# Taking PSUM banks in aligned pairs, with one instruction over two banks, in a two-layer attention and MLP kernel

## The chip, the cores and the metric

One core of one Trainium2 chip. The metric is the device time of one execution in microseconds (us), median of several.

The engines, as the profile names them: PE is TensorE's matmuls, PEld its weight loads, DVE is VectorE, ACT is ScalarE, POOL is GpSimd. The granted clock in a view is the share of its full clock at which TensorE ran.

## The reference

Two layers, each linear attention followed by a gated MLP, both on a layer norm of x and both added to x. x is 2048 x 576 in bf16 (16 tiles of 128 rows), 32 heads of 18, hidden width 4608.

```python
def _A_ref(x, wqkv, w_phi, wo):              # attention; shapes cut
    q, k, v = ...                            # x @ wqkv, split in heads of 18
    pq = einsum("bhsd,hdf->bhsf", q, w_phi)
    pk = einsum("bhsd,hdf->bhsf", k, w_phi)
    phi_q = concat([softmax(pq), softmax(-pq)])
    phi_k = concat([softmax(pk), softmax(-pk)])
    kv = einsum("bhsf,bhsd->bhfd", phi_k, v)
    z  = einsum("bhsf->bhf", phi_k)
    num = einsum("bhqf,bhfd->bhqd", phi_q, kv)
    den = einsum("bhqf,bhf->bhq", phi_q, z)[..., None] + 1e-6
    return (num / den) @ wo
def _B_ref(x, w_gate, w_up, w_down):         # the MLP
    return ((x @ w_gate) * (x @ w_up)) @ w_down

x = x + _A_ref(_layernorm(x), ...); x = x + _B_ref(_layernorm(x), ...)   # layer 1
x = x + _A_ref(_layernorm(x), ...); x = x + _B_ref(_layernorm(x), ...)   # layer 2
```

The softmax of -pk needs the minimum of each head where that of pk needs the maximum. This is where the two-bank instructions come in.

## The kernel before

The kernel is built by a greedy scheduler in Python. Tasks (`t_v`, `t_ain`, `t_down` and so on) ask for buffers and hand over lists of instructions; at each step the builder takes the instruction that can start first by its own table of durations. So **the order of the instructions on every engine follows from durations, priorities and the moment at which a task gets a buffer**.

PSUM is one pool `pb` of eight banks. A request for n banks gets those that came free longest ago:

```python
        names, n = r[1], r[2]
        cand = []
        for nm in names:
            p = self.pools[nm]
            for idx in p["free"]:
                cand.append((p["rel_time"][idx], nm, idx))
        if len(cand) < n:
            return False
        cand.sort()
        ...                                   # the first n of them
```

A bank counts as free once the builder has placed the instruction that reads it last. `rel_time` says when that instruction ends, which can lie ahead. A matmul into such a bank waits for that reader.

Layer 1 takes three banks at the very start for its kv sums and gives them back at the end of its attention. Five banks are left for everything else in this stage:

```python
    def t_layer1(self):
        gots = yield ("acqn", ["pb"], 3)
        s.kvb = [g_[1] for g_ in gots]
```

Who asks for what in that stage: a transpose or a product of the weight fuse (w_phi is multiplied into the k and q weights at the start) takes one bank, half a v projection takes one, a k projection takes two, for the two halves (288 wide each) of its row of 576:

```python
    def softmax_front(self, st_, pz, Wm, km, crit, ...):
        gots = yield ("acqn", ["pb"], 2, True)
        banks = [g_[1] for g_ in gots]
        yield from s.proj(st_, Wm, km, banks)            # the matmuls
        for h in range(2):                                # ACT: one cast for each bank
            yield ("ops", "act", [... e.copy(psb[:, pz, 288*h:288*h+288], s.ps[:, bank, 0:288]) ...])
        ops = [... e.tensor_reduce(mxmn[:, pz, 0, :], p3, AX.X, ALU.max) ...]
        for h in range(2):                                # DVE: one minimum for each bank
            ops.append(... e.tensor_reduce(mxmn[:, pz, 1, 16*h:16*h+16], pv, AX.X, ALU.min) ...)
        ...
        for h in range(2):                                # DVE: one subtraction for each bank
            ops.append(... e.tensor_tensor(d2h, pv, mnbh, ALU.subtract) ...)
        yield ("ops", "dve", ops)
        for bank in banks:
            yield ("rel", "pb", bank)
```

The scaling of a row by its layer norm (`xln`) may go to POOL or ACT in layer 1 and to DVE only on a fast path (six rows in all: two just ahead of each layer's first gate/up matmul, two between the layers):

```python
            yield ("alt", [(eng, [...]) for eng, dur in
                 (("pool", (800, 200)[:2 - fast]), ("dve", (400,)))[:1 + fast]] + ([("act", act)] if boot else []))
```

## Time and profile before

| | before |
|---|---|
| median of 3 runs | 1115.49 us |
| span of the profiled run | 1113.9 us |
| first Wk projection (k) on PE starts | 14.19 us |
| first gate/up matmul starts (layer 1's kv sums and its first rows of attention are done) | 117.8 us |
| last gate/up matmul of layer 1 starts | 599.5 us |
| first gate/up matmul of layer 2 starts | 653.3 us |

The busy shares, the busy time by stretch and the tail of the profile are shown in the prediction.

### The profile page before, as it was taken

How to read it: one execution, taken by the hardware profiler on the slowest of the kernel's cores; microseconds unless marked ns; L12 is line 12 of the kernel's file. 1: busy time of each engine (PE TensorE's matmuls, PEld its weight loads, DVE VectorE, ACT ScalarE, POOL GpSimd, SP SyncE). 2: the span in 40 equal slices, each digit the busy share in tenths (PEclk: the TensorE clock that was granted, in tenths of full speed). 3: DMA queues.
4: the chain of work that ended last, by engine and by line, in shares of the span. 5: the costliest groups of instructions: out<-in, count | busy, mean ns of one | idle time of the engine just before them, and what ended most of it. 6: DMA issues, size and time to landing. Idle time of an engine off the chain costs nothing.

```text
span 1113.9 us, 33734 instructions
## 1 busy us (share of the span) xinstructions
PE 1069.7 (96%) x15280; PEld 835.1 (75%) x15342; DVE 588.4 (53%) x1184; ACT 374.4 (34%) x862; POOL 313.3 (28%) x334
## 2 busy tenths in 40 slices
PE   5788999999999999999999899999999999999998
PEld 4565886868687786869687678696969696969685
DVE  7788744647375564646453675444535353524231
ACT  7786631414133241414232463131313030402120
POOL 4885512424152432413220252121212030300000
PEclk9899999999999999999999999999999999999999
DMA  8494227273542616371523313717272726362604
GB/s 175 114 314 157 32 47 197 47 204 47 151 97 79 158 39 186 47 204 26 152 75 98 96 24 47 214 36 215 35 215 35 205 46 191 58 180 49 179 26 139
DMA packets 185002, 129.07 MB, mean 116 GB/s; under 512 B 103322, under 2 KB 183706, under 8 KB 183706
## 3 DMA queue, kind: packets, MB, share of 16 engines
q1 hardware_dynamic: 184858, 126.91, 44.4%
q8 instruction: 120, 1.97, 0.7%
q14 instruction: 24, 0.20, 0.0%
HBM read 100.75 MB, written 2.36 MB: 93 GB/s over the span
## 4 chain that ended last, share of the span: by engine, by line
PE 83%; DVE 7%; ACT 4%; DMA 3%; POOL 2%; issue 1%; SPq 0%; DVEq 0%; POOLq 0%; ACTq 0%
PE ps L1427 47%; PE ps L1497 20%; PE ps L1001 6%; PE ps L1500 4%; PE ps L989 3%; PE ps L1288 2%; DMA wdr<-in_B_w_down_dram 1%; PE ps L1169 1%; DVE ss L1116 1%; DVE dd L1048 1%; POOL dd L1127 1%; ACT hT L1473 1%; DVE mxmn L1034 1%; DVE hT L1475 1%; DVE mxmn L1029 1%
## 5 line engine op out<-in xcount | busy, mean ns | idle before, releaser
L1427 PE MATMUL ps<-xT,Wu 64*128 64x256 bf16 x4608 | 582.2, 269 | 0.0
L1427 PE MATMUL ps<-xT,Wg 64*128 64x256 bf16 x4608 | 579.8, 269 | 0.8 <-ACT xT L971 0.8
L1427 PEld LDWEIGHTS ps<-xT,Wu 64*128 64x128 bf16 x4608 | 431.8, 94 | 22.4 <-DVE hT L1475 1.6
L1427 PEld LDWEIGHTS ps<-xT,Wg 64*128 64x128 bf16 x4608 | 427.2, 94 | 27.0 <-issue 3.3
L1473 ACT CAST hT<-ps 128x512 bf16<-128x512 f32 x288 | 168.0, 583 | 567.8 <-PE ps L1427 526.6
L1475 DVE TENSOR_TENSOR hT<-ps,hT 128x512 bf16<-128x512 f32 x288 | 196.9, 689 | 216.1 <-ACT hT L1473 215.3
L1497 PE MATMUL ps<-wdr,hT 128*128 128x512 bf16 x913 | 237.3, 380 | 0.9 <-DMA wdr<-in_B_w_down_dram 0.9
L1427 PE MATMUL ps<-xT,Wr 64*128 64x256 bf16 x1152 | 190.0, 269 | 0.0
L1500 PE MATMUL ps<-wdr,hT 128*128 128x64 bf16 x960 | 185.0, 193 | 3.1 <-DMA wdr<-in_B_w_down_dram 0.4
L1497 PEld LDWEIGHTS ps<-wdr,hT 128*128 128x128 bf16 x960 | 93.8, 98 | 110.8 <-DMA wdr<-in_B_w_down_dram 2.5
L1127 POOL TENSOR_TENSOR dd<-dd,ss 128x576 bf16<-128x576 bf16 x119 | 136.8, 1172 | 124.9 <-ACT ss L1123 121.0
L1098 POOL TENSOR_TENSOR dd<-xT,mxq 128x576 bf16<-128x576 bf16 x56 | 63.9, 1163 | 320.6 <-DVE mxq L1094 320.6
L1522 DVE TENSOR_TENSOR x_sb<-ps,x_sb 128x512 bf16<-128x512 f32 x32 | 22.0, 687 | 225.6 <-PE ps L1500 225.6
L961 POOL TENSOR_SCALAR xln<-x_sb,nmean,rstd 128x576 bf16<-128x576 bf16 x104 | 62.5, 607 | 172.9 <-ACT rstd L950 108.8
L1116 DVE TENSOR_REDUCE ss<-dd 128x64 f32<-128x1152 bf16 x61 | 82.1, 1347 | 31.6 <-ACT dd L1110 31.5
L1500 PEld LDWEIGHTS ps<-wdr,hT 128*128 128x128 bf16 x960 | 94.3, 98 | 0.0
L1427 PEld LDWEIGHTS ps<-xT,Wr 64*128 64x128 bf16 x1152 | 82.8, 94 | 5.2
L1108 ACT ACTIVATE dd<-dd 128x576 bf16<-128x576 bf16 x61 | 41.7, 684 | 47.6 <-DVE dd L1048 30.9
L1039 POOL TENSOR_TENSOR dd<-psb,mxmn 128x576 bf16<-128x576 bf16 x26 | 30.2, 1163 | 80.6 <-DVE mxmn L1029 80.6
L1497 PE MATMUL ps<-wdx,hT 128*128 128x512 bf16 x177 | 50.8, 380 | 0.0
L933 DVE BATCH_NORM_STATS2 st<-x_sb 128x6 f32<-128x288 bf16 x120 | 46.0, 446 | 2.8 <-DMA x_sb<-in_A_x_dram 2.7
L1001 PE MATMUL ps<-Wo,oT 64*128 64x288 bf16 x504 | 44.0, 283 | 0.8
(123 smaller groups left out, 968.9 us busy)
## 6 DMA issues: line engine op xcount, KB each, us to landing
wdr<-in_B_w_down_dram SPq DMA_DIRECT2D x240, 288.0 KB, 3.5
wdx<-in_B_w_down_dram SPq DMA_DIRECT2D x48, 288.0 KB, 3.4
Wg<-in_B_w_gate_dram SPq DMA_DIRECT2D x4, 1152.0 KB, 16.4
Wu<-in_B_w_up_dram SPq DMA_DIRECT2D x4, 1152.0 KB, 18.5
x_sb<-in_A_x_dram SPq DMA_DIRECT2D x8, 288.0 KB, 3.1
out_dram<-x_sb SPq DMA_DIRECT2D x16, 144.0 KB, 2.3
Wraw<-in_A_wqkv_dram SPq DMA_DIRECT2D x8, 144.0 KB, 2.8
xT<-xln SPq DMA_TRANSPOSE x58, 2.6
```

Of the source, the lines that this page charges most:

```text
L933: ops.append(Op(d_dve(288), (lambda e, j=j, h=h, src=src: e.bn_stats(st[:, sl[j], 6 * h:6 * h + 6], src)), reads=rd, writes=[("st", sl[j], ...
L961: em = [(lambda e, j=j, a=a, b=b, c=c: e.tensor_scalar(xln[:, sl[j], a:b], x_sb[:, ss[j], c:c + b - a], s.nmean[:, sl[j]:sl[j] + 1], rstd[ ...
L1001: out.append(Op(61, (lambda e, h=h, k=k, st=(i == 0 and k == 0), sp=(i == 1 and k == 3): e.matmul(s.ps[:, banks[h], 0:N], L[r, k, :], Wm[r ...
L1098: yield ("ops", "pool", [Op(1150, (lambda e, d=d, mb=mb: e.tensor_tensor(d, p3, mb, ALU.subtract)), reads=[("xT", st_), ("mq", mq, br)], w ...
L1108: yield ("ops", "act", [Op(590, (lambda e: e.activation(de2, de2, ACTF.Exp, scale=-1.0)), reads=s.ddk(sm, 1), writes=s.ddk(sm, 1))])
L1116: Op(1320, (lambda e: e.tensor_reduce(ss[:, sm, :].rearrange("p (b g) -> p b g", b=2), e4, AX.X, ALU.add)), reads=s.ddk(sm, 0) + s.ddk(sm, ...
L1127: yield ("alt", [(eng, [Op(dur, (lambda e, ev=ev, rb=rb: e.tensor_tensor(ev, ev, rb, ALU.mult)), reads=s.ddk(sm, br) + [("ss", sm)], write ...
L1427: out.append(Op(54.3, (lambda e, bank=bank, cs=cs, lhsT=lhsT, rhs=rhs, st=st, sp=sp: e.matmul(ps[:, bank, cs].rearrange("p (a n) -> p a n" ...
L1473: yield ("ops", "act", [Op(540, (lambda e, gb=gb, p=p: e.copy(hT[:, p, :], ps[:, gb, :])), reads=[("gu", gb)], writes=[("hT", p)] + (s.raw ...
L1475: yield ("ops", "dve", [Op(625, (lambda e, ub=ub, p=p: e.tensor_tensor(hT[:, p, :], ps[:, ub, :], hT[:, p, :], ALU.mult)), reads=[("gu", u ...
L1497: ops.append(Op(d_pe(512), (lambda e, lhsT=lhsT, bank=bank, slot=slot, fi=fi, f=f: e.matmul(ps[:, bank, 0:512], lhsT, s.wslot(slot)[:, fi, ...
L1500: ops.append(Op(d_pe(64) + 3, (lambda e, lhsT=lhsT, sl=sl, slot=slot, fi=fi, f=f: e.matmul(ps[:, Z, 64 * sl:64 * sl + 64], lhsT, s.wslot(s ...
```

## The change

The intent: fewer, longer DVE and ACT instructions. Banks 2i and 2i+1 are adjacent in PSUM, so one instruction can read both. To have such a pair, banks are given by a new rule, and with it come four more edits. The diff, cut to its core:

```diff
+        if names[0] == "pb":
+            got = self._banks(r[2] if r[0] == "acqn" else 1)
+            if got is None:
+                return False
+    def _banks(self, n):
+        p = self.pools["pb"]
+        free, rel = set(p["free"]), p["rel_time"]
+        got = []
+        while n >= 2:                         # the pair demand
+            pairs = [i for i in range(0, 8, 2) if i in free and i + 1 in free]
+            if not pairs:
+                return None
+            i = min(pairs, key=lambda i: max(rel[i], rel[i + 1]))
+            got += [i, i + 1]
+            free -= {i, i + 1}
+            n -= 2
+        if n:                                 # the single rule
+            if not free:
+                return None
+            i = min(free, key=lambda i: ((i ^ 1) in free, rel[i]))
+            got.append(i)
+        return got
 ...
-        self.fq = 3                           # when the q weight is fused
-        self.fqs = 2
+        self.fq = 1
+        self.fqs = 1
 ...                                           # DVE may scale rows in layer 1
-  ("dve", (400,)))[:1 + fast]] + ...
+  ("dve", (400,) if fast else (400, 200)))[:1 + (fast or boot)]] + ...
 ...                                           # merges; the same for q cast, den, multiply, adds to x
-        for h in range(2):
-            ... e.copy(psb[:, pz, 288*h:288*h+288], s.ps[:, bank, 0:288])
+        pv = s.two(banks, 288)                # = self.ps[:, banks[0]:banks[0] + 2, 0:288]
+        ... e.copy(psb[:, pz, :].rearrange("p (t n) -> p t n", t=2), pv)
-        for h in range(2): ops.append(Op(370, ... ALU.min ...))
+        ops.append(Op(690, (lambda e: e.tensor_reduce(mn3, pv4, AX.X, ALU.min)), ...))
 ...                                           # last down phase: the last 3 chunks tile by tile
+        NR = NF - CH * s.NLAST * last
+        for sl in range(2):
+            for f in range(NR, NF):
+                yield ("ops", "pe", mm(f, sl))
+            if sl == 0 and last:
+                yield ("go", s.t_bepi(L, b, 0, X, ZZ[0], True), 11, "bepi%d" % b)
```

Below, its parts are called the **pair demand** (two banks must be an aligned pair), the **single rule** (a single bank is taken where its partner is taken, whenever that bank comes free), the **merges**, the **split** (of the last down phase, which also takes a fourth bank; the 64 wide add of a tile now comes before the 512 wide one), the **norms** (rows scaled by DVE in layer 1) and the **early fuse**.

## The prediction

> **What bounds the kernel now.** I read the page's busy shares first, then busy time by stretch, then the groups by shape, then the timeline at the three places where TensorE waits, and the chain that ended last.
>
> ```profile
> PE 1069.7 (96%) x15280; PEld 835.1 (75%) x15342; DVE 588.4 (53%) x1184; ACT 374.4 (34%) x862; POOL 313.3 (28%) x334
> ```
>
> TensorE is busy for 96% of the span and no other engine is near that. So what an instruction on VectorE or ScalarE costs matters only where TensorE waits for it. I cut the span by what TensorE does: attention of layer 1 ahead of the first gate/up matmul (0 to 117.85), gated block of layer 1, the passage between the layers (619 to 653.3), gated block of layer 2. Columns: stretch, its length, then busy us with instruction counts of PE, weight loads, DVE, ACT, POOL, then granted clock, DMA share, GB/s.
>
> ```profile
> 14.00:28.00 14.00, 10.83 (x69) 7.18 (x70) 12.85 (x38) 10.71 (x33) 7.74 (x10) 0.87 0.87 155
> 28.00:56.00 28.00, 20.56 (x169) 14.42 (x166) 22.20 (x47) 19.88 (x53) 22.34 (x23) 0.83 0.46 113
> 56.00:84.00 28.00, 23.73 (x221) 18.22 (x222) 24.48 (x44) 22.98 (x64) 24.95 (x23) 0.94 0.96 317
> 84.00:103.30 19.30, 14.88 (x124) 10.62 (x122) 17.78 (x31) 13.32 (x34) 11.38 (x10) 0.91 0.36 139
> 103.30:117.85 14.55, 13.91 (x139) 10.26 (x137) 10.96 (x27) 9.09 (x23) 4.50 (x5) 1.00 0.34 107
> 118.00:618.00 500.00, 497.39 (x7487) 388.55 (x7514) 271.87 (x537) 157.81 (x365) 149.58 (x158) 1.00 0.44 108
> 619.00:653.30 34.30, 28.87 (x268) 22.21 (x266) 26.50 (x59) 20.06 (x52) 9.58 (x8) 1.00 0.08 24
> 653.30:1084.00 430.70, 427.37 (x6477) 342.24 (x6506) 187.06 (x365) 107.92 (x216) 77.08 (x82) 1.00 0.45 113
> ```
>
> The two gated stretches hold 930.7 us, of which TensorE idles 2.61 + 3.33 = 5.9: nothing that shortens DVE or ACT work can gain more there. Between 14 and 103.3 us DVE is 87% busy (77.3 of 89.3), POOL 74% and TensorE 78% at a clock of 0.83 to 0.94: there VectorE, with GpSimd close behind in the middle, sets the pace. In the passage TensorE idles 5.4 of 34.3 us, behind a serial chain through DVE, ACT and POOL. After the last matmul (begun at 1109.63) come the adds and the store, some 4 us. These three places hold all there is to win.
>
> **What the Trainium skill says.** "Perfetto Trace Analysis", section Optimizing Scalar/DVE Operations, gives a data-access overhead per instruction of about 125 ns for DVE on PSUM and 51 ns for ScalarE on PSUM; it says that grouping helps a saturated engine, and that splitting may help one that is not saturated but causes bubbles elsewhere. Both halves bear on this change. The trace gives less for DVE than 125 ns (next part) and about as much for ACT. "PSUM — Partial Sum Buffer", section Terms, has one bank as 2 KiB per partition and one matmul output within one bank: the matmuls stay as they are, and two adjacent banks are one regular pattern for a reader. No run so far shows that such a read costs nothing extra; I assume it.
>
> **Cost of one merge.**
>
> ```profile
> L1363 DVE TENSOR_TENSOR x_sb<-ps,x_sb 128x288 bf16<-128x288 f32 x56 | 25.4, 454 | 6.0 <-PE ps L1001 4.9
> L1522 DVE TENSOR_TENSOR x_sb<-ps,x_sb 128x512 bf16<-128x512 f32 x32 | 22.0, 687 | 225.6 <-PE ps L1500 225.6
> L1473 ACT CAST hT<-ps 128x512 bf16<-128x512 f32 x288 | 168.0, 583 | 567.8 <-PE ps L1427 526.6 <-PE ps L1001 39.0
> L1026 ACT CAST psb<-ps 128x288 bf16<-128x288 f32 x56 | 20.4, 400 | 18.7 <-PE ps L1001 15.3 <-PE ps L989 3.4
> ```
>
> DVE: (687-454)/224 = 1.04 ns per element, so 576 elements should take 687 + 64 x 1.04 = 753 ns. ACT: (583-400)/224 = 0.82, so 583 + 52 = 635 ns. Against these stand pairs as the timeline has them (start, length of both, group):
>
> ```profile
> 626.55 0.81 DVE L1048 TENSOR_TENSOR dd<-ps,mxmn 128x288 bf16<-128x288 f32 x2
> 628.55 0.68 ACT L1026 CAST psb<-ps 128x288 bf16<-128x288 f32 x2
> ```
>
> Two back to back overlap, so a pair is 0.81, not 0.89, on DVE and 0.68, not 0.80, on ACT. A merge saves 0.055 us of DVE and 0.045 us of ACT, far less than a whole instruction. It also loses something: a cast of bank 1 began while bank 2 was still filling, so where a cast is on the path, 0.40 after the last matmul becomes 0.64.
>
> **Part by part.** The instruction lists of both builds (neither times anything) say what moves.
>
> 1. Layer 1 up to the gated block. DVE: 36 minima and 36 subtractions become 18 and 18: -36 x 0.055 = -2.0 us. Seven of the 16 normalisations (rows of 576 and 64; 0.43 us from the 576 row, and I take 0.15 for the 64) move to DVE: +4.1. Three weight casts leave it, -1.2. In sum about +0.9 us for DVE. POOL loses three normalisations of 0.82 + 0.39 us, -3.6; ACT loses four of 0.87 + 0.29 + 0.24, -5.6, and about -1.0 from merged casts. The moved work lands before 50 us, where DVE has some room (12.85 of 14, 22.2 of 28) and POOL less. So the merges hardly relieve the bound engine; it is the balance that gets better. DVE idles 12.0 us from 14 to 103.3, in part behind ACT and POOL. I choose 1.5 us of that as regained. At the end one q projection fewer stands before the first gate/up matmul, so that this waits for the last cast of xT (116.59 + 0.69) rather than for TensorE at 117.85: -0.5. Together -2.0.
> 2. That q projection, and one from the passage, go into the first gated block of each layer. A layer-2 block lasts 57.04 us (chain, gate/up starts at 771.95 and 828.99): 9 x 4.04 gate/up, 72 x 0.245 down, 2 x 0.62 attention numerator; 1.8 remains for two projections on half rows, 0.9 each. So +1.8 for the two.
> 3. Passage. Three chunks of two rows, six steps of one tile, 6 x 0.245 = 1.5 us of matmuls now stand behind tile 0's end, so its add and layer norm start 1.5 earlier. The new list puts tile 1's adds between tile 0's mean and its normalisation: tile 0's scaling starts near 620.2, not 621.40: -1.2. The merged cast gives 0.24 back: -1.0 at the softmax, and everything is serial from there to the kv matmuls at 637.68. Then transposes of tile 0 go ahead of tile 1's numerator (0.62): -0.6. One q projection less in front of the last transposes: -0.4. Together -2.0.
> 4. End. In
>
> ```profile
> 1109.58 0.69 DVE L1522 TENSOR_TENSOR x_sb<-ps,x_sb 128x512 bf16<-128x512 f32 x1 [16.13 <-PE ps L1500]
> 1110.19 0.21 DVE L1524 TENSOR_TENSOR x_sb<-ps,x_sb 128x64 bf16<-128x64 f32 x1
> 1110.32 0.68 DVE L1522 TENSOR_TENSOR x_sb<-ps,x_sb 128x512 bf16<-128x512 f32 x1
> 1110.92 0.21 DVE L1524 TENSOR_TENSOR x_sb<-ps,x_sb 128x64 bf16<-128x64 f32 x1
> ```
>
> all four adds come behind TensorE. Now only one 512 wide add does: 1109.85 (last matmul done, my estimate) + 0.69 = 1110.55 in place of 1111.13: -0.6.
>
> The other merges (denominator, multiply, adds, q casts inside gated blocks) lie beside a TensorE that does not wait: 0. Sum: -2.0 + 1.8 - 2.0 - 0.6 = -2.8. The constants that moved too (when the q weight is fused, normalisations allowed on DVE) look like the order being tuned again for the new lengths; for that I take 1.2 us more. 1115.49 - 4.0 = 1111.5.
>
> **Rivals.** (a) Aligned pairs run short. Layer 1 keeps three banks for kv through its attention; five remain, two pairs and a single, and a single v projection that breaks a pair would make a k projection wait while two banks are free. For it: TensorE waits on releases by casts there already. Against: singles take the odd bank first, and before it needed two of five as well. It would add 2 to 5 us in layer 1: 1114 to 1117. (b) A two-bank read costs DVE extra, or the casts' lost overlap is felt at each tile: 16 x 0.24 = 3.8 us more at worst, which eats the gain: 1115. (c) DVE stays the bound in layer 1 and the moved normalisations lengthen it by their 0.9 us; passage and end still gain: about 1114. (d) Balance is worth more than I took: all 12 us of DVE idling can't go, but half can: 1106.
>
> **Range and chances.** The three runs before spread by 2.8 us, so 1 us either way is the median's own. With (d) at one end and (a) to (c) at the other: 1106 to 1115.5. Faster by over 2% needs 1093.2, 22 us off, more than half of all TensorE idling: 0.02. Slower by 2% needs 1137.8, thus pair shortage in the gated blocks, whose matmul order is unchanged but for two projections: 0.01.
>
> **What would show it.** Right: merged DVE instructions of 0.74 to 0.77 us and casts of 0.63 to 0.65; first gate/up matmul at 115 to 116.5; passage near 32 us, end of matmuls to end of span 0.6 shorter; PE busy total within 3 us of 1069.7; gated stretches idle as before. Wrong: the first gate/up after 118 with TensorE waiting for DVE releases (a); merged instructions over 0.80 (b); idle over 8 us in the gated stretches.

## More of the kernel before

A change in how buffers are given moves instructions all over the stage.

One view that the prediction did not show belongs here. It is the timeline of PE at the start: start, length, line and operation, output and inputs, count, and in brackets the idle time before and what ended it.

```profile
5.21 1.33 PE L835 MATMUL ps<-ident,Wraw 128*126 128x128 bf16 x10 [5.21 <-DMA Wraw<-in_A_wqkv_dram]
7.07 0.64 PE L887 MATMUL ps<-BDphi,WT 126*128 126x126 bf16 x5 [0.53 <-ACT WT L838]
7.51 0.77 PE L835 MATMUL ps<-ident,Wraw 128*126 128x128 bf16 x5
...
14.19 2.56 PE L989 MATMUL ps<-Wk,xT 128*128 128x288 bf16 x10 [1.93 <-ACT Wk L900]
```

L835 are transposes of the raw weight, five to a bank. Ten of them run in one go, into two banks, and PE does not wait for the cast (L838) of the first bank before it fills the second.

## The result, and the profile after

The changed kernel takes 1121.53 us (median of 4 runs, 1120.37 to 1122.29), the kernel before 1114.97 us in the runs beside it (4 runs, 1113.39 to 1117.24). The ratio is 1.0056, 95% interval 1.0036 to 1.0077: within 2%, but slower by some 6 us, where 4 us less had been forecast, and outside the range.

| start on PE, profiled runs | before | after | difference |
|---|---|---|---|
| first Wk projection | 14.19 | 17.80 | +3.6 |
| first gate/up matmul | 117.8 | 124.6 | +6.8 |
| first gate/up matmul of layer 2 | 653.3 | 660.5 | +7.2 |
| end of span | 1113.9 | 1120.3 | +6.4 |

So **the whole loss lies ahead of the first gate/up matmul**, and half of it is there at 17.8 us. The granted clock does not explain it: up to the first gate/up matmul it was 0.91 before and 0.96 after. The page's first line and the busy time by stretch after (columns as in the prediction):

```profile
PE 1075.7 (96%) x15358; PEld 816.6 (73%) x15358; DVE 578.8 (52%) x1023; ACT 369.4 (33%) x797; POOL 311.0 (28%) x328
```

```profile
0.00:14.00 14.00, 5.29 (x38) 3.80 (x38) 7.54 (x26) 7.00 (x17) 3.57 (x15) 1.00 0.69 186
14.00:28.00 14.00, 9.97 (x62) 6.34 (x62) 11.91 (x30) 8.30 (x22) 6.16 (x8) 1.00 0.52 101
56.00:84.00 28.00, 20.39 (x169) 13.92 (x167) 26.84 (x41) 18.75 (x48) 19.09 (x18) 0.94 0.79 249
84.00:103.30 19.30, 15.41 (x140) 10.89 (x138) 18.64 (x22) 14.83 (x35) 16.22 (x15) 1.00 0.54 225
0.00:124.50 124.50, 90.29 (x750) 63.27 (x750) 101.22 (x180) 80.36 (x195) 76.29 (x83) 0.96 0.58 170
124.60:627.40 502.80, 501.95 (x7544) 385.17 (x7545) 265.07 (x467) 159.18 (x343) 147.92 (x156) 1.00 0.44 108
```

and two stretches of the kernel before that the prediction did not show:

```profile
0.00:14.00 14.00, 5.45 (x50) 4.71 (x50) 8.88 (x31) 9.60 (x24) 5.96 (x19) 0.98 0.74 192
0.00:117.85 117.85, 89.36 (x762) 65.42 (x764) 97.14 (x213) 85.57 (x226) 76.87 (x88) 0.91 0.63 180
```

161 DVE instructions are gone and 9.6 us of its busy time. But up to the first gate/up matmul DVE is busy for 101.2 us where it had been 97.1. By its account, 4.1 of the 6.8 us lost there are more work and 2.7 are more idling, though which instructions fall before that mark differs a little. In the gated stretch PE idles 0.85 of 502.8 us, so nothing is lost there. In the first 14 us PE got 38 instructions instead of 50, though nothing in this stretch is merged. The timeline of PE there after the change:

```profile
5.36 0.79 PE L865 MATMUL ps<-ident,Wraw 128*126 128x128 bf16 x5 [5.36 <-DMA Wraw<-in_A_wqkv_dram]
7.12 0.80 PE L865 MATMUL ps<-ident,Wraw 128*126 128x128 bf16 x5 [0.97 <-ACT WT L868]
...
11.46 0.79 PE L865 MATMUL ps<-ident,Wraw 128*126 128x128 bf16 x5 [0.80 <-ACT WT L868]
...
17.80 2.58 PE L1019 MATMUL ps<-Wk,xT 128*128 128x288 bf16 x10 [0.41 <-ACT Wk L930]
```

The transposes now come five at a time, and the second five wait 0.97 us for the cast of the first five: both go into the same bank. The banks that the two builders gave, in order, show why:

```
before: kv [0,1,2]; then singles 3 4 5 6 7 3 4 5 6 3 7 4 5 6 3;   first k [4,7]
after:  kv [0,1,2]; then singles 3 3 4 3 3 5 6 3 7 3 3 4 5 3 3;   first k [6,7]
```

Bank 3 is the one whose partner is held by the kv sums, so the single rule always likes it best, even while its reader is still at work: it is 9 of the 15 singles after and 4 before.

The merged instructions came out as forecast. The groups by shape (busy us, mean ns of one):

```profile
L1383 DVE TENSOR_TENSOR x_sb<-ps,x_sb 128x576 bf16<-128x576 f32 x28 | 21.0, 751 | 8.7 <-PE ps L1031 8.7
L1062 DVE TENSOR_REDUCE mxmn<-ps 128x32 f32<-128x576 f32 x28 | 20.9, 748 | 0.0
L1056 ACT CAST psb<-ps 128x576 bf16<-128x576 f32 x28 | 17.9, 638 | 21.4 <-PE ps L1031 13.4 <-PE ps L1019 7.9
```

A DVE merge is 0.75 us (forecast 0.753) and a cast 0.638 (0.635). The timeline of DVE shows what this saves, and where it goes:

```profile
33.69 0.74 DVE L1058 TENSOR_REDUCE mxmnx<-psbx 128x32 f32<-128x576 bf16 x1
34.35 0.74 DVE L1062 TENSOR_REDUCE mxmnx<-ps 128x32 f32<-128x576 f32 x1
35.02 0.73 DVE L1058 TENSOR_REDUCE mxmnx<-psbx 128x32 f32<-128x576 bf16 x1
...
42.30 0.75 DVE L1058 TENSOR_REDUCE mxmn<-psb 128x32 f32<-128x576 bf16 x1 [4.55 <-ACT psb L1056]
```

The merged minimum takes 35.02 - 34.35 = 0.67 us from start to start, a pair before took 626.55 - 625.82 = 0.73. But two tiles' minima come together, and then DVE stands still for 4.55 us for the cast of the next k projection. At this place DVE waits. Later it does not: from 56 to 103.3 us it is busy for 26.84 + 18.64 = 45.5 of 47.3 us (96%; before 24.48 + 17.78 = 42.3, 89%), so there DVE still sets the pace, more than before.

The norms came out dearer than forecast. Before, DVE has only the six 576-wide rows of the fast path (2.6 us, 428 to 429 ns each); after:

```profile
L991 DVE TENSOR_SCALAR xln<-x_sb,nmean,rstd 128x576 bf16<-128x576 bf16 x13 | 7.2, 554 | 2.8 <-ACT rstd L980 2.8
L991 DVE TENSOR_SCALAR xln<-x_sb,nmean,rstd 128x64 bf16<-128x64 bf16 x7 | 5.0, 719 | 0.3
```

The seven that moved cost 7.2 - 2.6 + 5.0 = 9.6 us, not 4.1: 64 elements take longer than 576 do at best. POOL is at work beside them at those times. Three of the seven come late, where DVE has no room:

```profile
60.51 1.46 DVE L991 TENSOR_SCALAR xln<-x_sb,nmean,rstd 128x576 bf16<-128x576 bf16 x2
64.69 3.47 DVE L991 TENSOR_SCALAR xln<-x_sb,nmean,rstd 128x576 bf16<-128x576 bf16 x4
```

The Trainium skill, "SBUF — State Buffer", section Who interferes with whom, says that DVE in a 2-port mode and GpSimd exclude each other for a whole instruction; that fits the lines of the seven, but run a4 below could not confirm it.

The end, timeline of DVE:

```profile
1115.11 0.23 DVE L1564 TENSOR_TENSOR x_sb<-ps,x_sb 128x64 bf16<-128x64 f32 x1 [14.73 <-PE ps L1523]
1115.31 0.69 DVE L1562 TENSOR_TENSOR x_sb<-ps,x_sb 128x512 bf16<-128x512 f32 x1
1116.58 0.22 DVE L1564 TENSOR_TENSOR x_sb<-ps,x_sb 128x64 bf16<-128x64 f32 x1 [0.57 <-PE ps L1523]
1116.78 0.69 DVE L1562 TENSOR_TENSOR x_sb<-ps,x_sb 128x512 bf16<-128x512 f32 x1
```

Tile 0's adds are over before PE ends (last matmul 1116.36 + 0.38 = 1116.74), as intended. From there to the end of the span it is 3.56 us, before it was 1113.9 - (1109.63 + 0.19) = 4.08: 0.5 us gained.

### The profile page after: what moved, and what is told of

It reads as the page before. It is cut to its first block, busy times and chain, and to the rows that moved or that the text cites. A ratio compares the mean times of both kernels' runs of the same rounds, so it can differ in the third digit from the quotient of the medians.

```text
span 1120.3 us, 33573 instructions
## 1 busy us (share of the span) xinstructions
PE 1075.7 (96%) x15358; PEld 816.6 (73%) x15358; DVE 578.8 (52%) x1023; ACT 369.4 (33%) x797; POOL 311.0 (28%) x328
## 4 chain that ended last, share of the span: by engine, by line
PE 85%; DVE 5%; DMA 3%; ACT 1%; POOL 0%; issue 0%; SPq 0%
PE ps L1448 50%; PE ps L1521 20%; PE ps L1031 7%; PE ps L1523 3%; PE ps L1312 2%; DMA wdr<-in_B_w_down_dram 2%; PE ps L1019 1%; DVE ss L1140 1%; PE ps L1193 1%; DVE dd L1071 1%; DMA oT<-dd 1%; DMA wdx<-in_B_w_down_dram 0%; DVE xln L991 0%; DVE mxmn L1062 0%; POOL dd L1151 0%; DVE mxmn L1058 0%
## 5 line engine op out<-in xcount | busy, mean ns | idle before, releaser
L1521 PE MATMUL ps<-wdr,hT 128*128 128x512 bf16 x960 | 245.9, 380 | 1.3 <-DMA wdr<-in_B_w_down_dram 1.1
L1448 PE MATMUL ps<-xT,Wr 64*128 64x256 bf16 x1152 | 162.5, 269 | 0.0
L1564 DVE TENSOR_TENSOR x_sb<-ps,x_sb 128x64 bf16<-128x64 f32 x32 | 7.0, 220 | 234.2 <-PE ps L1523 234.2
L991 POOL TENSOR_SCALAR xln<-x_sb,nmean,rstd 128x576 bf16<-128x576 bf16 x98 | 59.7, 615 | 178.3 <-ACT rstd L980 173.0
L1448 PEld LDWEIGHTS ps<-xT,Wr 64*128 64x128 bf16 x1152 | 61.1, 94 | 6.8
L1132 ACT ACTIVATE dd<-dd 128x576 bf16<-128x576 bf16 x61 | 41.6, 682 | 44.7 <-DVE dd L1071 35.9
L1521 PE MATMUL ps<-wdx,hT 128*128 128x512 bf16 x192 | 54.3, 380 | 0.1
L1134 ACT ACTIVATE dd<-dd 128x576 bf16<-128x576 bf16 x61 | 41.0, 671 | 0.0
## 6 DMA issues: line engine op xcount, KB each, us to landing
Wg<-in_B_w_gate_dram SPq DMA_DIRECT2D x4, 1152.0 KB, 14.2
```

Source lines behind the costliest of these rows:

```text
L991: em = [(lambda e, j=j, a=a, b=b, c=c: e.tensor_scalar(xln[:, sl[j], a:b], x_sb[:, ss[j], c:c + b - a], s.nmean[:, sl[j]:sl[j] + 1], rstd[ ...
L1132: yield ("ops", "act", [Op(590, (lambda e: e.activation(de2, de2, ACTF.Exp, scale=-1.0)), reads=s.ddk(sm, 1), writes=s.ddk(sm, 1))])
L1448: out.append(Op(54.3, (lambda e, bank=bank, cs=cs, lhsT=lhsT, rhs=rhs, st=st, sp=sp: e.matmul(ps[:, bank, cs].rearrange("p (a n) -> p a n" ...
L1521: ops = [Op(d_pe(512), (lambda e: e.matmul(s.ps[:, bank, 0:512], lhsT, s.wslot(slot)[:, fi, 0:512], start=(f == 0), stop=(f == NF - 1))), ...
```

## The experiments

Eighteen kernels were run. First their results in one table, then each group with its edits and expectations. "Wk", "g/u" and "g/u end" are the starts, in the profiled run, of the first Wk projection, the first gate/up matmul and the last gate/up matmul of layer 1. Each run was timed beside the kernel before on the same chip (medians there 1114.08 to 1115.34 us).

| run | what it is | median us | ratio to before (95%) | Wk | g/u | g/u end |
|---|---|---|---|---|---|---|
| before | | 1114.97 | 1 | 14.2 | 117.8 | 599.5 |
| after | all parts | 1121.53 | 1.0056 (1.0036 to 1.0077) | 17.8 | 124.6 | 607.6 |
| a1 | after, no norms | 1125.77 | 1.0092 (1.0076 to 1.0109) | 19.3 | 128.5 | 611.9 |
| a2 | after, old fuse | 1122.40 | 1.0062 (1.0047 to 1.0077) | 17.7 | 127.1 | 609.1 |
| a3 | after, neither | 1125.69 | 1.0087 (1.0072 to 1.0102) | 19.3 | 127.9 | 610.1 |
| a4 | after, norms strided | 1122.41 | 1.0062 (1.0047 to 1.0077) | 18.0 | 125.8 | 608.7 |
| b4 | before + bank rule | 1127.70 | 1.0123 (1.0106 to 1.0140) | 19.4 | 128.7 | 611.0 |
| b5 | before + split | 1111.82 | 0.9981 (0.9966 to 0.9996) | 13.9 | 117.5 | 598.2 |
| a5 | a3, adjacent pairs | 1143.83 | 1.0270 (1.0254 to 1.0285) | 16.9 | 135.3 | 611.2 |
| a6 | a3, old banks | 1112.16 | 0.9984 (0.9969 to 0.9999) | 14.1 | 119.0 | 599.2 |
| c1 | a3, pair preferred | 1130.55 | 1.0137 (1.0123 to 1.0151) | 19.3 | 135.2 | 616.4 |
| c2 | b4, rule only late | 1117.17 | 1.0027 (1.0014 to 1.0040) | 14.3 | 116.9 | 600.4 |
| c3 | a3, rule only late | 1113.45 | 0.9988 (0.9976 to 1.0000) | 14.5 | 116.9 | 599.9 |
| c4 | a6 + norms + fuse | 1117.57 | 1.0026 (1.0014 to 1.0038) | 15.7 | 124.1 | 603.9 |
| d1 | before + single rule | 1125.33 | 1.0090 (1.0077 to 1.0103) | 19.5 | 127.0 | 608.8 |
| d2 | before + pair demand | 1118.05 | 1.0029 (1.0016 to 1.0041) | 14.4 | 122.0 | 603.5 |
| d3 | after, oldest single | 1122.57 | 1.0070 (1.0058 to 1.0083) | 15.4 | 124.9 | 608.9 |
| d4 | after, ready single | 1123.78 | 1.0072 (1.0056 to 1.0088) | 15.6 | 123.4 | 607.2 |
| e1 | a6 + norms | 1118.43 | 1.0039 (1.0027 to 1.0052) | 15.3 | 124.0 | 604.3 |
| e2 | a3, oldest single | 1122.42 | 1.0066 (1.0051 to 1.0081) | 14.0 | 132.2 | 611.1 |

Medians differ by up to 1 us where ratios agree; read the ratios for small differences. "0.1% of ratio" is 1.1 us.

### Are the norms or the early fuse the loss? (a1, a2, a3, a4)

The first theory was the norms, dearer by 5.5 us than forecast; the second the early fuse, which puts more into the start. (The 10.5 us in a1's expectation are 9.6 by the lines above.)

a1 sets this back in the changed kernel, a2 the two constants, a3 both:

```diff
-  ("dve", (400,) if fast else (400, 200)))[:1 + (fast or boot)]]
+  ("dve", (400,)))[:1 + fast]]                                     # a1, a3
-        self.fq = 1
-        self.fqs = 1
+        self.fq = 3                                                 # a2, a3
+        self.fqs = 2
```

> The changed kernel, only with VectorE taken out of the choice for layer 1's normalisations again. Theory 1 (the seven normalisations on VectorE are what lengthened layer 1: they took 10.5 us of VectorE, not the 4.1 forecast, because they collide with GpSimd): the first gate/up matmul comes back from 124.6 to about 118, the time to about 1115. Theory 2 (fusing the q weight earlier delays the k and v projections): still about 1120. Theory 3 (aligned pairs run short): still about 1120.

> The changed kernel, only with the two constants that say when the q weight is fused set back to 3 and 2. Theory 2: the 4.6 us stall of VectorE near 38 us goes and the time falls to about 1116. Theory 1: five normalisations of 576 stay on VectorE (seven before), so at most a third of the loss comes back, about 1119 to 1120. Theory 3: 1121.

> The changed kernel with both set back, so only the merged instructions, the aligned pairs and the split of the last down phase are left. If pairs cost nothing: first gate/up matmul at 115 to 117, passage 33 us, end 0.5 shorter, about 1112. Theory 3 (pairs run short): first gate/up matmul at 121 or later, about 1118.

Both theories fall as the whole cause. Without the norms the kernel is slower still (ratio 1.0092 against 1.0056), with the old fuse it is no better (1.0062). With both set back it is 1.0087: so pairs, merges and split together cost some 10 us, and beside them the two constants together give about 3 to 4 us back (0.0031 of ratio, a3 to after).

a4 keeps the order of all instructions and lets the moved norms read and write every second element, in two rows of half the length, in the hope that this form does not keep DVE and POOL apart:

```diff
+  evn = lambda t: t.rearrange("p (n two) -> p two n", two=2)
+  ... e.tensor_scalar(evn(xln[...]), evn(x_sb[...]), ...)          # DVE, layer 1 only
```

> The changed kernel with the same order of instructions on every engine; only the access pattern of VectorE's normalisations in layer 1 is changed, so that even elements are done ahead of odd ones[...]. Theory 1: the rows of 576 take about 0.67 us each and those of 64 about 0.2 instead of 0.72 on average, VectorE gains some 3.5 us, the first gate/up matmul comes 2 to 4 us earlier, about 1118. Theories 2 and 3: no change beyond 1 us.

It did not do what it was built for, and nothing shows that this form is free of the lock at all: the seven 576-wide rows took 875 ns and the 64-wide ones 744 ns, together 11.3 us instead of 9.6, and the total is 1.0062. So whether the lock between DVE and POOL makes the norms dear stays open. The run is of use in another way: it is the only one that leaves the order alone, and with 1.7 us more of DVE time in this stage the first gate/up matmul came 1.2 us later (one trace each), as it should where DVE sets the pace.

### Is it the pairs? (b4, b5, a5, a6)

b4 is the kernel before with `_banks` and nothing else, so no merges. b5 is the kernel before with the split alone.

> The kernel before, with only the rule for taking banks changed to aligned pairs; all instructions stay one bank wide. Theory 3 (aligned pairs run short while three of eight banks are held for kv): the first gate/up matmul at 124 or later, about 1121 to 1125. Theory 4 (the merged instructions hurt: a cast starts only when both banks are full, and a pair is held until its last reader): no change, about 1115.

> The kernel before with only the last down phase of each layer split by tile. Both theories: layer 1 as before (first gate/up matmul at 117.9), passage 1 us and end 0.5 us shorter, about 1113.5. If the passage gained through something else, no change in it.

b4: ratio 1.0123, 13.7 us slower, with the first gate/up matmul at 128.7. The bank rule by itself costs more than twice what the whole change loses. b5: ratio 0.9981, 2.1 us faster (0.4 to 3.8), and the lowest median of all runs, though a6 and c3 cannot be told from it.

a5 (a3, but any two adjacent banks are a pair, in the hope that more pairs can be had) and a6 (a3's code with the banks of the kernel before, merged only where two banks happen to lie side by side, 9 of all 36 minima):

```diff
-  pairs = [i for i in range(0, 8, 2) if i in free and i + 1 in free]
+  pairs = [i for i in range(7) if i in free and i + 1 in free]      # a5
-  i = min(free, key=lambda i: ((i ^ 1) in free, rel[i]))
+  i = min(free, key=lambda i: ((i - 1 in free) + (i + 1 in free), rel[i]))
```

> The changed kernel with the two scheduling choices set back, and pairs that need only be adjacent, not aligned: with banks 0 to 2 held for kv, banks 3 to 7 now offer four pairs in place of two. Theory 3: part of the loss comes back, first gate/up matmul at 120 to 124 in place of 127.9, about 1118 to 1121. Theory 4: as with aligned pairs, 1125.

> As the last one, but banks are taken as in the kernel before, whichever were released longest ago, and two banks are read by one instruction only where they happen to be adjacent (5 of 18 minima in layer 1's attention). Theory 3: layer 1 is as in the kernel before or a little shorter, about 1112 to 1114. Theory 4: about 30 percent of the loss stays, 1117.

a5 missed its expectation by far: 1.0270. Among banks 3 to 7 a pair 4-5 leaves 3, 6, 7, and a pair 5-6 leaves 3, 4, 7 with no pair at all; the run shows the loss, not that this is its cause. a6 gives 0.9984, the same as b5. With the old choice of banks, the split and the few merges that this choice allows are at least harmless.

### Where, and is it the demand? (c1, c2, c3, c4)

Theory 3 at this point was the prediction's rival (a): a k projection waits for an aligned pair while two other banks are free. c1 takes the demand away and keeps the preference (by its profile 33 of all 36 minima of k and q are merged; the 25 of 28 in its expectation leave out eight that write to a second tile); c2 and c3 confine the rule to the time after layer 1 has given back its kv banks; c4 adds the two constants to a6.

```diff
             if not pairs:
-                return None
+                if len(free) < n:                                   # c1
+                    return None
+                return got + sorted(free, key=lambda i: rel[i])[:n]
 ...
-        if names[0] == "pb":
+        if names[0] == "pb" and self.late:                          # c2, c3
```

> The changed kernel's merged code with its split end, old constants, and its rule for banks with one difference: an aligned pair is preferred, not demanded. If none is free, any two free banks are taken and the instructions stay single; 25 of the 28 minima come out merged. Singles still avoid breaking a pair. Theory 3 (the demand for an aligned pair makes k projections wait with two banks free): the demand is gone, so 1110 to 1114, first gate/up matmul at 115 to 118.5. Rival 3b (what costs is the choice: a single that takes an odd bank instead of the one released longest ago waits for it, and so do pairs): the choice is still made, so 1119 to 1126 as in a3, first gate/up at 123 or later.

> The kernel before with the aligned-pair rule (no merges), but only from the moment that layer 1's three kv banks are given back; until then banks are taken as before. Theory 3 with its place (five banks in layer 1's attention): 1113 to 1116, as before, first gate/up matmul at 117.3 to 118.5, against 1127.7 with the rule throughout. If the rule also costs in the gated blocks or the passage: 1118 or more, with the first gate/up still at 118.

> The changed kernel's merged code, split end and old constants; banks are taken as before until layer 1's kv banks are given back (merged only where two happen to lie side by side), in aligned pairs after that, so nearly all merges of the gated blocks and the passage are there. Theory: those merges lie beside a TensorE that doesn't wait, but for the passage, so 1110.5 to 1113, at most 1 us below the 1112.2 of a6. If the merges of the passage are worth the 0.2 to 1 us a tile that a serial chain would pass on: 1108 to 1110. If the late pair rule costs: 1114 or more.

> a6 (any two banks, merged where they happen to lie side by side, split end) with the changed kernel's two constants on top: VectorE may do normalisations in layer 1, and the q weight is fused early. If these balance the engines by themselves, as I forecast (1.2 us and part of 1.5): 1109 to 1111.5. If they only helped a kernel starved of banks (3 to 4 us there, since a normalisation on VectorE lets a waiting engine work): 1111.5 to 1115, no gain over a6.

c1 breaks theory 3 as the whole cause: without the demand it is slower still, 1.0137, and its first Wk projection is as late (19.3) as with it. Something costs before any k projection asks for a pair. c2 shows the place: with the rule only after layer 1's attention, the first gate/up matmul is at 116.9, and of a loss of 1.23% (b4) 0.27% remains. So most of it is in layer 1's attention, and some 3 us are not, more than theory 3 with its place had left over. c3 has nearly all merges of the gated blocks and the passage and is no faster (0.9988) than a6 (0.9984), which has few: those merges are worth nothing that the runs can tell, as the prediction had it. c4 was a surprise: the constants, which gave 3 to 4 us back beside the bank rule, cost 4.7 us (1.0026 against 0.9984) without it.

### Which half of the rule? (d1, d2, d3, d4)

d1 and d2 are the halves alone on the kernel before; d3 and d4 are the changed kernel with one line changed.

```diff
-            i = min(free, key=lambda i: ((i ^ 1) in free, rel[i]))
+            i = min(free, key=lambda i: rel[i])                     # d2, d3: oldest
+            i = min(free, key=lambda i: (max(rel[i], self.free_at["pe"]), (i ^ 1) in free, rel[i]))   # d4
-        while n >= 2: ...                                           # d1: any two banks
+        if n >= 2:
+            return sorted(free, key=lambda i: rel[i])[:n] if len(free) >= n else None
```

> The kernel before with only one half of the aligned-pair rule: a request for one bank prefers a bank whose partner is taken, no matter when it comes free; a request for two takes any two. In the built program the first transposes then take bank 3 again and again, where the kernel before goes round banks 3 to 7. Theory 6 (this reuse costs: TensorE waits each time for the reader of bank 3; in the run with pairs only the first Wk projection begins at 19.4 us instead of 14.2): 1122 to 1128, first gate/up matmul at 124 to 130, first Wk projection near 19. Theory 3 (the demand for an aligned pair costs): 1113 to 1117, as before.

> The other half alone, on the kernel before: two banks must be an aligned pair, a single takes the bank that came free longest ago, as before. Theory 6: the start is as before (first Wk projection at 14.2 to 15), 1113 to 1118. Theory 3: 1121 to 1128, with k projections waiting for a pair.

> The changed kernel with one edit: a single takes the bank that came free longest ago, whether it breaks a pair or not. Theory 6: the 5 us of the start come back, first gate/up at 117 to 120, total 1112 to 1117. Theory 3 (breaking pairs makes k projections wait, which the preference was there to avoid): 1122 or more.

> The changed kernel with one edit: a single is chosen among the banks that will be free by the time that TensorE can write, and among those it spares a pair; only if none is free by then does it take the next to come free. Theory 6: no wait of the start is left and pairs are spared, 1109 to 1115, no slower than the run with the oldest single. Theory 3: 1118 to 1123, as the changed kernel.

d1: 1.0090, so **the single rule alone costs 10 us**. d2: 1.0029, the pair demand alone 3 us. The waits of PE in the first 28 us (line, what it waited for, total us, times, longest) in d1:

```profile
PE ps L857 <- ACT WT L860: 2.5, 3, 1.0
PE ps L909 <- DVE Wk L922: 2.1, 2, 1.7
PE ps L909 <- ACT WT L860: 1.7, 2, 1.0
```

and all that d2 has of the same kind (there L915 is the product of the weight fuse, L909 in d1):

```profile
PE ps L915 <- ACT WT L866: 1.4, 2, 0.8
```

L857 is the transpose that waits for the cast of its own bank, 2.5 us in all in d1 and absent in d2 and in the kernel before. With the waits of the product that follows it makes 6.3 us against 1.4, and the first Wk projection comes 5.3 us later than before (19.5 against 14.2). This part of the cause is shown; it is 5.3 of the 9.2 us by which d1's first gate/up matmul is late, and the rest is not traced. In d1, d2 and b4 alike DVE is busy for 96.9 to 97.2 us up to that matmul, as before (97.1): what the bank rules cost is waiting, not work. Which wait makes up d2's 3 us no trace shows. The Trainium skill says it in advance: "Perfetto Trace Analysis", section Optimizing Tensor Performance (Matmuls), "Independent matmul groups should rotate through different PSUM banks so the ACT/DVE evacuation of one overlaps the next group's matmuls". The trace agrees, with these numbers.

But d3 and d4 did not give it back. Their first Wk projection comes 2.2 to 2.4 us earlier than in the changed kernel, their first gate/up matmul at 124.9 and 123.4 (124.6), and their ratios are 1.0070 and 1.0072, no better than 1.0056. Mending the start is not enough: something else holds the first gate/up matmul at 123 to 125. The expectation that the 5 us come back is refuted.

### What is the second limit? (e1, e2)

e1 is a6 with the norms only; e2 is d3 with both constants set back, thus d2 plus merges and split.

> a6 (any two banks, merged where they happen to lie side by side, split end) with one of the two constants: VectorE may do normalisations in layer 1. a6 had 1112.2 and its first gate/up matmul at 119.0, both constants together 1117.6 and 124.1. If the normalisations on VectorE cost (two instructions of some 0.5 us each, beside GpSimd): 1115.5 to 1118.5, first gate/up at 122 to 125. If the early fuse of the q weight costs: 1110.5 to 1113.5, first gate/up at 117.5 to 120.

> The changed kernel with three edits: a single takes the bank that came free longest ago, and both constants are set back. It is the pair demand of d2 (1118.05, first gate/up at 122.0) plus merges and the split end. If the three causes add up (single rule, constants, pair demand) and merges are worth what I forecast at most: 1118.05 less 2.1 for the split and 0 to 1 for the merges, so 1114 to 1117 with the first gate/up at 121 to 123. If the constants help as they did beside the single rule (1125.7 to 1121.5), taking them out makes it slower than d3's 1122.6: 1123 to 1127.

e1: 1.0039 and a first gate/up matmul at 124.0, against 0.9984 and 119.0 for a6. So it is the norms, by 6 us, where banks are given as before, together with the new order that they bring (e1 happens to merge 23 of the 36 minima, a6 9); the early fuse on top of them changes nothing that can be told (c4, 1.0026, 124.1). In e1 DVE has 13 scalings of 538 ns and seven of 500 in place of six of 428: 7.9 us more on the engine that is busiest in this stage. Up to the first gate/up matmul DVE is busy for 104.7 us in e1 and 95.7 in a6: the norms cost work, where the bank rules cost waiting.

e2 missed: 1.0066, with a first gate/up matmul at 132.2, 10 us later than in d2, which differs only by the merges up to there. Its timeline of PE shows a new picture:

```profile
55.64 1.40 PE L1019 MATMUL ps<-Wk,xT 128*128 128x288 bf16 x10 [1.01 <-DVE dd L1071]
...
57.49 1.39 PE L1019 MATMUL ps<-Wk,xT 128*128 128x288 bf16 x10
61.56 1.38 PE L1019 MATMUL ps<-Wv,xT 128*128 128x288 bf16 x5 [2.69 <-ACT vxx L1178]
```

and its timeline of DVE at the same time:

```profile
59.43 2.61 DVE L1140 TENSOR_REDUCE ss<-dd 128x64 f32<-128x1152 bf16 x2 [2.98 <-ACT dd L1134]
```

Two k projections have taken both pairs, from 55.6 and 57.5 us, and hold them through casts, minima and subtractions. A v projection has bank 3 alone and its second half waits 2.69 us for the cast of the half before it, which stands behind the norms and exponentials of ACT; DVE in its turn waits 2.98 us for those. Two tiles go in step, and each engine works in bursts. In the kernel before, k projections took what two banks there were (first [4, 7], then [6, 3]). Merging should add to this, since a bank can't be read until its partner is full; that it does so here is not shown.

The merges, however, have no cost of their own that the runs would agree on. From b4 to a3 merges and split came, and the ratio fell by 0.0036, of which b5's split explains 0.0019; from d2 to e2 the same two came, and it rose by 0.0037.

## Why the prediction was wrong

Its steps, measured on the traces:

- **Step 1, layer 1 up to the gated block: wrong in sign, +6.8 instead of -2.0.** It is most of the miss: 8.8 of the 10.4 us between the forecast -4.0 and the +6.4 of the two spans. It failed at two sentences.
  - The first is in rival (a), which I put aside with "singles take the odd bank first, and before it needed two of five as well". The first half of this was read as a protection. It is the costliest part: the single rule alone costs 10 us (d1), of which 5.3 come from taking the odd bank again while its reader works. That needed no pair to be short. I looked at who waits for a pair and not at how often a single gets the same bank. The order of bank grants was there to be read, and so was the skill's sentence on rotating banks. The second half was wrong as well: as an aligned pair, two of five cost 3 us (d2), though no trace names the wait.
  - The second is the norms: "the balance that gets better", 1.5 us regained and part of the 1.2. Without the bank rule they cost 6 us (e1); they were sized at 0.43 + 0.15 us each, and came out at 0.66 + 0.72 in the changed kernel. "The moved work lands before 50 us" failed too: three of the seven came at 60.5 to 68.2 us, in a stretch where DVE is 96% busy. DVE's work up to the first gate/up matmul grew by 4.1 us and not 0.9, and its idling grew by 2.7 where 1.5 regained had been forecast. So rival (c), DVE stays the bound and the norms lengthen it, came true in part, at four times its size.
- **The merges' durations: right,** 0.75 and 0.638 us, and with them the sentence that a merge saves only some 0.06 us. What was missing is that DVE, "the pace" of this stage, can be made to wait: after, it stands still for 4.55 us at once behind a cast, and from 56 us on it has no slack to make that up.
- **Step 2, q projections in the gated blocks: the move was right, its size only in the sum.** One projection more is in each layer's block. Layer 1's, from the first gate/up matmul to the passage, takes 502.9 us (627.42 less 124.56) instead of 501.2 (618.95 less 117.78), +1.7. Layer 2's, to the end of the last matmul, takes 456.2 instead of 456.5, -0.3. Together +1.4, against 0.9 for each. PE's busy total, forecast within 3 us, rose by 6.0; some of this is records that the trace before lacks (15280 matmuls for 15342 weight loads; after, 15358 for both).
- **Step 3, passage (33.1 us for 34.3): mechanism right, size -1.2 instead of -2.0.** The scaling of tile 0 begins 1.35 us after the end of the down phase instead of 2.45, as forecast; the 0.6 and 0.4 us from later orders did not show. With the split alone (b5) the passage is 33.2 us, so the split gives 1.1 of the 1.2 and the merges next to nothing.
- **Step 4, end: right,** -0.5 for -0.6; b5 has passage and end together in the total, -2.1 us.
- **The constants, "1.2 us more": wrong.** What they are worth depends on the rest: -3 to -4 us beside the rule (a3 to after), +4.7 without it (a6 to c4).

Why do the parts not add up? Alone, the single rule costs 10 us and the pair demand 3 (on the kernel before) and the norms 6 (on a6); the whole change, which has all three and a split that gains 2, loses 6.5. A reading that fits, but is argued and not shown: the stage ends where its latest engine ends, each of the three makes another engine late (PE waits for a cast of bank 3, k for a pair, DVE has more to do), and while one of them is the last, taking away another gives nothing: a1, a2, d3 and d4 each mend one thing in the changed kernel, and none is faster. The versions as fast as the kernel before or faster (a6, c3, b5) all have neither the rule in layer 1 nor the norms.

**What stays open.** Every edit of the rule also gives another order of some hundred instructions, as the builder takes them greedily. Apart from the start, where the wait for bank 3 is seen line by line, and the norms, whose added work is seen on DVE, no run separates the rule's own waits from the luck of the order that comes with it; e2, slower where the sum said faster, and the merges without a stable sign, suggest that this luck is worth several us. How the 6.5 us of the change divide among its parts is therefore not settled, and neither is what makes a 64-wide scaling take 0.72 us.

**The version to keep** is the kernel before with the split alone: 1111.82 us, ratio 0.9981 (0.9966 to 0.9996).

## What to carry to other kernels

Before you give buffers by a new rule, write down the sequence in which they are given and look for one that comes back while it is still being read: a preference that ignores when a buffer comes free came back to one bank of five for 9 of the first 15 grants. A merge here saved 0.06 us, and a rule that makes merging possible has to cost less than that in waits. Where a stage has several engines near their limit, a test that mends one part in the changed kernel can show nothing, and a test that adds one part to the kernel before shows each cost; do both.

## What the Trainium skill lacked or had wrong

- "Perfetto Trace Analysis", section Optimizing Scalar/DVE Operations: its 125 ns of access overhead for DVE on PSUM is not what a merge saves. A pair of 288 wide minima took 0.81 us from the first start to the last end and the merged one 0.75, so about 0.06 us. For ACT, where the page has 51 ns, a pair of casts took 0.68 us and the merged one 0.64.
- The same page, section Matmuls, has the advice on rotating banks, but no size: with three of eight banks held, steering singles to one bank made a start of 14.2 us one of 19.5 (d1; that kernel was 0.9% slower in all).
- No page speaks of demanding adjacent banks from a pool of which some are held: with five left, it cost 0.3% for aligned pairs alone (d2), and 2.7% where any two adjacent banks made a pair and singles spared them, with merges and split on top (a5).
- "SBUF — State Buffer", section Who interferes with whom, explains why DVE and GpSimd hold each other up, but not how to see in a profile that it happened. The 64 wide scaling took 719 ns beside GpSimd, and with a stride of two elements 744 (a4); neither number says whether the lock was held.
